# Experts with 416 places instead of 384: a fourth tile of 32 rows for each expert, and two overflow tiles instead of six

## The chip, the cores and the metric

The kernel runs on one core of one Trainium2 chip. The metric is the device time of one execution in microseconds (us), as the median of several runs. Engines are named as in the profile: PE is TensorE's matmul, PEld its weight load, DVE VectorE, ACT ScalarE, POOL GpSimd, SP SyncE.

## The reference

The first half is clustered attention over 4 batches, 8 heads, 768 positions and 64 dimensions. It gives 3072 rows of 512. The second half is a mixture of 8 experts in which each row goes to exactly one expert, and no row is dropped:

```
logits = x @ w_gate                       # x: 3072 x 512, w_gate: 512 x 8
expert_idx = np.argmax(logits, axis=1)
...
for e in range(E):                        # the rows of expert e
    h = np.maximum(x_sorted[lo:hi] @ w1[e], 0.0)   # w1[e]: 512 x 1024
    y_sorted[lo:hi] = h @ w2[e]                    # w2[e]: 1024 x 512
y = y_sorted[inv_perm]
return gate_w[:, None] * y
```

Everything is float32. How many rows an expert gets depends on the data. With the reference's inputs the eight experts get 400, 354, 531, 257, 408, 444, 274 and 404 rows.

## The kernel before

The attention stage (lines 252 to 581) works through 16 groups of a batch and two heads. Its order on each engine is written out by hand. Several of its matmuls use a part of the PE array only: `similar` (L362) puts four products of 32 output columns into four quarters of one PSUM tile, `weigh` (L463) puts two such products into two quarters and adds three rounds up, `weigh2` (L477) transposes blocks of 64 rows. The attention writes its rows, with the gate weight in a further column, to a table `x_rows` in device memory.

The routing stage (L584 to L713) counts the rows of each expert and gives each row a place. Each expert has `CAP` = 384 places, three tiles of 128. Rows beyond that go to overflow tiles of 128 rows that belong to one expert each. A product of one-hot matrices (L703) turns the places around into a table `g_idx` (for each tile a column with the numbers of the rows to be gathered) and `s_idx` (the rows of the output to be written; empty places point out of bounds and are not written). The count of overflow tiles is a value at run time; the first `XU` = 6 are written out in the program, and a loop (L797 to L807) does any further one.

The expert stage takes the groups in the order experts 0 to 7, then overflow tiles 0 to 5. For a group, `gather` fetches its rows by an indirect DMA for each tile (POOL), `turn_rows` transposes them on PE (4 transposes for a tile into `tp`, two buffers, emptied by DVE), `layer1` computes `h` for all tiles of the group at once (32 matmuls into `hp`, moving 384 columns, or 128 for an overflow tile), and `layer2` takes one tile after the other (8 matmuls of 512 columns into `zp`, two buffers, emptied by ACT with the gate weight, then an indirect DMA on POOL to the output). The order on PE is written out: layer 1 of group i, transposes of group i+1, layer 2 of group i. After them come the gather of group i+2 and the fetch of the weights of group i+3, two transfers of 2 MB on SP's queue into one of three weight buffers.

A float32 matmul stands in the trace as two records, a transpose as one.

Of the kernel before, what the change touches and what calls it, by code (L numbers as in the profile page):

```python
# [8 lines left out]
F32 = mybir.dt.float32  # L9
# [3 lines left out]
AF = mybir.ActivationFunctionType  # L13
# [6 lines left out]
BIG = float(2**60)  # L20
LAG = 2
LEAD = 14
XU = 6


def in_general(tc, ident, ident_b, first_c, first_e, wpool, q, k, v, centroids, w_gate, w1, w2, out):
# [156 lines left out]
def kernel(  # L183
# [11 lines left out]
    nc = tc.nc  # L195
    B, H, S, D = q.shape
    C = centroids.shape[1]
    P = 128
# [5 lines left out]
    N = B * S  # L204
    Dm = H * D
    E = moe_w_gate.shape[1]
    F = moe_w1.shape[2]
    DB = Dm // P
    FB = F // P
    NT = N // P  # L210
    KA = D + C
    XW = Dm + 4
    assert D == 64 and C == 16 and H * C == P and NQ % 2 == 0 and NQ * P == S and DB * P == Dm and FB * P == F

    NJ = N // E // P
    CAP = NJ * P
    NX = -(-(N - CAP) // P)
    NC = E * NJ + NX
    assert XU <= NX

    x_d = nc.dram_tensor("x_rows", (N, XW), F32, kind="Internal").ap()

    consts = ctx.enter_context(tc.tile_pool(name="consts", bufs=1))
# [3 lines left out]
    def fetch(e):  # L227
        w1 = wpool.tile([P, DB, F], F32, name="w1")
        w2 = wpool.tile([P, FB, Dm], F32, name="w2")
        nc.sync.dma_start(out=w1, in_=moe_w1[bass.ds(e, 1)].rearrange("e (a p) f -> p (e a) f", p=P))  # L230
        nc.sync.dma_start(out=w2, in_=moe_w2[bass.ds(e, 1)].rearrange("e (a p) d -> p (e a) d", p=P))
        return w1, w2
# [19 lines left out]
    with ExitStack() as actx:  # L252
# [4 lines left out]
        ap = actx.enter_context(tc.tile_pool(name="ap", bufs=4))  # L257
# [9 lines left out]
        rows = {}  # L267
# [34 lines left out]
        for i in range(2):  # L302
            t = consts.tile([P, 2 * NQ, 2, D], BF16, name=f"oh{i}")
# [289 lines left out]
    keep = consts.tile([P, E, NT], F32)  # L593
    nc.gpsimd.memset(keep, 1.0)
    nc.gpsimd.memset(keep[:, :, 0:1], 0.0)
    b1off = iota("b1off", [P, E], [[CAP, E]], -1, 0)
    b2off = iota("b2off", [P, E], [[-CAP, E]], E * CAP - CAP, 0)
    thr = iota("thr", [P, NX], [[P, NX]], CAP, 0)
    kx = iota("kx", [1, NX], [[1, NX]], 0, 0)
    iota_f = iota("iota_f", [P, P], [[1, P]], 0, 0)  # L600
    tokv = iota("tokv", [P, B, NQ], [[S, B], [1, NQ]], 1, NQ)

    g_idx = rte.tile([P, NC], I32)
    s_idx = rte.tile([P, NC], I32)
    xe = rte.tile([1, NX + 2], I32)

    with tc.tile_pool(name="sm", bufs=1) as sm, tc.tile_pool(name="rps", bufs=1, space=PSUM) as rps:
# [59 lines left out]
        gx = sm.tile([P, E, NT], F32)  # L667
        nc.vector.tensor_scalar(gx, slot, scalar1=CAP + 0.5, scalar2=None, op0=ALU.is_ge)
        nc.vector.tensor_tensor(gx, gx, b2.unsqueeze(2).to_broadcast([P, E, NT]), op=ALU.mult)
# [14 lines left out]
        oh_r = sm.tile([P, NT, P], F32)  # L684
        oh_c = sm.tile([P, NT, NC], F32)
        tok_ps = rps.tile([P, NC], F32, name="tok_ps")
        tok = tokv.rearrange("p b j -> p (b j)")
        TH = NT // 4
        for t0 in range(0, NT, TH):
            ts = slice(t0, t0 + TH)  # L690
            nc.vector.tensor_tensor(
                oh_c[:, ts, :], iota_f[:, None, :NC].to_broadcast([P, TH, NC]),
                rc[:, 1, ts].unsqueeze(2).to_broadcast([P, TH, NC]), op=ALU.is_equal,
            )
# [18 lines left out]
        nc.vector.tensor_copy(s_idx, tb)  # L713


    mctx = ExitStack()
    xg_pool = mctx.enter_context(tc.tile_pool(name="moe_x", bufs=3))
    wk = mctx.enter_context(tc.tile_pool(name="moe_wk", bufs=2))
    mps = mctx.enter_context(tc.tile_pool(name="moe_ps", bufs=3, space=PSUM))

    def gather(g):
        g["xg"] = xg_pool.tile([P, NJ, XW], F32, name="xg")
        for j in range(g["n"]):
            nc.gpsimd.indirect_dma_start(  # L724
                out=g["xg"][:, j, :], out_offset=None,
                in_=x_d[:, :], in_offset=bass.IndirectOffsetOnAxis(ap=g["gi"](j), axis=0),
            )

    def turn_rows(g):
        g["xT"] = wk.tile([P, DB, NJ * P], F32, name="xgT")  # L730
        for j in range(g["n"]):
            tp = mps.tile([P, DB, P], F32, name="tp", bufs=2)
            for c in range(DB):
                nc.tensor.transpose(tp[:, c, :], g["xg"][:, j, c * P : (c + 1) * P], ident)  # L734
            nc.vector.tensor_copy(g["xT"][:, :, j * P : (j + 1) * P], tp)  # L735

    def layer1(g):
        cols = g["n"] * P
        g["h"] = wk.tile([P, FB, NJ * P], F32, name="h_sb")
        for fb in range(FB):  # L740
            hp = mps.tile([P, NJ * P], F32, name="hp")
            for c in range(DB):
                nc.tensor.matmul(  # L743
                    hp[:, :cols], lhsT=g["w"][0][:, c, fb * P : (fb + 1) * P], rhs=g["xT"][:, c, :cols],
                    start=(c == 0), stop=(c == DB - 1),
                )
            if fb % 2 == 0:
                nc.vector.tensor_relu(g["h"][:, fb, :cols], hp[:, :cols])  # L748
            else:
                nc.scalar.activation(g["h"][:, fb, :cols], hp[:, :cols], AF.Relu)  # L750

    def layer2(g):
        for j in range(g["n"]):
            zp = mps.tile([P, Dm], F32, name="zp", bufs=2)
            for fb in range(FB):
                nc.tensor.matmul(  # L756
                    zp, lhsT=g["h"][:, fb, j * P : (j + 1) * P], rhs=g["w"][1][:, fb, :],
                    start=(fb == 0), stop=(fb == FB - 1),
                )
            zo = wk.tile([P, Dm], F32, name="zo", bufs=3)  # L760
            nc.scalar.activation(zo, zp, AF.Copy, scale=g["xg"][:, j, Dm : Dm + 1])  # L761
            ins = nc.gpsimd.indirect_dma_start(  # L762
                out=out[:, :], out_offset=bass.IndirectOffsetOnAxis(ap=g["si"](j), axis=0),
                in_=zo, in_offset=None, bounds_check=N - 1, oob_is_err=False,
            )
            if g["apart"]:
                ins = getattr(ins, "ins", ins)
                tc.declare_no_dep(ins, group="rows_out", reason="disjoint rows")
                tc.add_to_no_dep_group("rows_out", ins)

    def cols_of(t, c0):
        return lambda j: t[:, c0 + j : c0 + j + 1]

    groups = []
    for e in range(E):
        groups.append(dict(n=NJ, e=e, gi=cols_of(g_idx, e * NJ), si=cols_of(s_idx, e * NJ), apart=True))
    for x in range(XU):
        ex = nc.sync.value_load(xe[0:1, x : x + 1], min_val=0, max_val=E - 1)
        groups.append(dict(n=1, e=ex, gi=cols_of(g_idx, E * NJ + x), si=cols_of(s_idx, E * NJ + x), apart=True))
    with tc.manual_schedule():  # L780
        for i in range(2):
            gather(groups[i])
        turn_rows(groups[0])
        for i, g in enumerate(groups):
            g["w"] = weights.pop(i)
            layer1(g)
            if i + 1 < len(groups):
                turn_rows(groups[i + 1])
            layer2(g)
            if i + 2 < len(groups):  # L790
                gather(groups[i + 2])
            if i + 3 < len(groups):
                weights[i + 3] = fetch(groups[i + 3]["e"])

    nx = nc.values_load(xe[0:1, NX : NX + 1], min_val=0, max_val=NX)
    general = nc.values_load(xe[0:1, NX + 1 : NX + 2], min_val=0, max_val=1)
    with tc.If(nx > XU):  # L797
        with tc.For_i(XU, nx, 1) as i:
            ex = nc.sync.value_load(xe[0:1, bass.ds(i, 1)], min_val=0, max_val=E - 1)
            gi = wk.tile([P, 2], I32, name="gi")  # L800
            nc.vector.tensor_copy(gi[:, 0:1], g_idx[:, bass.ds(i + E * NJ, 1)])
            nc.vector.tensor_copy(gi[:, 1:2], s_idx[:, bass.ds(i + E * NJ, 1)])
            g = dict(n=1, w=fetch(ex), gi=lambda j: gi[:, 0:1], si=lambda j: gi[:, 1:2], apart=False)
            gather(g)
            turn_rows(g)
            layer1(g)
            layer2(g)  # L807
# [31 lines left out]
```

## Time and profile before

| | us |
|---|---|
| median of 3 runs (942.52 to 944.6) | 943.83 |
| the profiled execution | 942.97 |
| span of its profile, first to last instruction | 941.1 |
| PE busy | 880.3 |
| PE's weight load busy (beside PE) | 454.3 |
| DVE busy | 302.1 |
| ACT busy | 270.8 |
| POOL busy | 93.2 |

The profile describes one execution; its span is 1.9 us shorter than that execution's time, and the execution is 0.9 us shorter than the median. Busy time of an engine is the union of its instructions. The span divides by stage: attention up to about 449 us, routing and first gather up to 483 us, eight experts up to 829 us, six overflow tiles up to 931 us, and an end of 10 us in which the last rows are written and the two conditions behind the groups are read.

### The profile page before, as it was taken

The numbers are of one execution on the slowest core, as the hardware profiler recorded it, in microseconds if no ns is written. First come the engines' busy times: TensorE is split into PE (matmuls) and PEld (weight loads), VectorE is DVE, ScalarE is ACT, GpSimd is POOL, SyncE is SP. The second block draws the span as 40 slices with busy tenths as digits, with TensorE's granted clock in tenths as the row PEclk, the third lists the DMA queues.
The fourth block names the chain that finished last, engine by engine and source line by source line (L and its number), as shares of the span: only waits on it lengthen the run. The fifth ranks groups of instructions, "written<-read, shape, count | busy, mean of one in ns | idle before, by whom it ended". The sixth has DMA issues, their size and how long they took to land.

```text
span 941.1 us, 10715 instructions
## 1 busy us (share of the span) xinstructions
PE 880.3 (94%) x4367; PEld 454.3 (48%) x4367; DVE 302.1 (32%) x527; ACT 270.8 (29%) x432; POOL 93.2 (10%) x141
## 2 busy tenths in 40 slices
PE   4999999999999999999479999999999999989895
PEld 2444444444444444444445555454545455556663
DVE  2565556555554556554611010100101010001110
ACT  3645455555554555454000101001000101101110
POOL 3000000000000000000220202010120201011000
PEclk8999999999999999999669999999999999989998
DMA  7127223151235322000122424232434333256700
GB/s 159 29 52 229 51 51 119 65 174 42 51 119 207 73 51 85 2 1 1 67 68 92 155 100 144 111 135 112 154 125 180 125 126 121 100 212 217 275 18 11
DMA packets 82587, 99.00 MB, mean 105 GB/s; under 512 B 52959, under 2 KB 57055, under 8 KB 82016
## 3 DMA queue, kind: packets, MB, share of 16 engines
q1 hardware_dynamic: 76480, 77.60, 26.2%
q0 software_dynamic: 5376, 20.56, 5.7%
q8 instruction: 37, 0.61, 0.3%
q14 instruction: 22, 0.18, 0.1%
q10 hardware_dynamic: 672, 0.05, 0.0%
HBM read 85.57 MB, written 14.20 MB: 106 GB/s over the span
## 4 chain that ended last, share of the span: by engine, by line
issue 44%; PE 40%; DVE 7%; POOL 6%; ACT 1%; DMA 0%; POOLq 0%; DVEq 0%; ACTq 0%
PE sps L425 14%; PE O L445 12%; PE mps L463 4%; DVE T L437 3%; PE sps L428 3%; POOL out_dram L762 3%; POOL xg L724 3%; PE mps L342 2%; PE mps L362 1%; ACT A L430 1%; PE tok_ps L703 1%; PE mps L400 1%; DVE qk L350 1%; PE mps L373 1%; PE mps L506 1%
## 5 line engine op out<-in xcount | busy, mean ns | idle before, releaser
L743 PE MATMUL hp<-xgT,w 128*128 128x384 f32 (+1 forms) x896 | 212.2, 398 | 0.8 <-DVE xgT L735 0.8
L756 PE MATMUL zp<-w,h_sb 128*128 128x512 f32 x480 | 211.7, 600 | 0.0
L430 ACT ACTIVATE A<-sps 128x768 f32<-128x768 f32 x192 | 155.4, 811 | 80.4 <-PE sps L428 78.7
L743 PEld LDWEIGHTS hp<-xgT,w 128*128 128x128 f32 x896 | 142.1, 192 | 73.8 <-issue 7.9
L425 PE MATMUL sps<-qk 64*128 64x384 f32 x768 | 166.1, 510 | 0.0
L437 DVE TENSOR_TENSOR T<-T,A 128x768 f32<-128x768 f32 x128 | 122.5, 957 | 85.6 <-ACT A L430 78.6
L445 PE MATMUL O<-A,v_in 128*64 128x384 f32 x768 | 145.1, 499 | 0.0
L756 PEld LDWEIGHTS zp<-w,h_sb 128*128 128x128 f32 x480 | 91.7, 194 | 110.0 <-issue 110.0
L748 DVE TENSOR_SCALAR h_sb<-hp 128x384 f32<-128x384 f32 (+1 forms) x56 | 24.9, 444 | 358.9 <-PE hp L743 358.9
L425 PEld LDWEIGHTS sps<-qk 64*128 64x128 f32 x768 | 63.4, 187 | 52.2 <-issue 31.5
L445 PEld LDWEIGHTS O<-A,v_in 128*64 128x64 f32 x768 | 46.6, 136 | 79.8 <-issue 79.8
L750 ACT ACTIVATE h_sb<-hp 128x384 f32<-128x384 f32 (+1 forms) x56 | 22.3, 399 | 215.3 <-PE hp L743 215.3
L761 ACT ACTIVATE zo<-zp,xg 128x512 f32<-128x512 f32 x30 | 20.6, 687 | 221.3 <-PE zp L756 221.3
L762 POOL DMA_INDIRECT out_dram<-zo,s_idx x30 | 30.1, 1002 | 389.9 <-ACT zo L761 389.9
L428 PE MATMUL sps<-ohT 64*128 64x384 bf16 x384 | 63.2, 323 | 0.0
L433 DVE SCALAR_TENSOR_TENSOR T<-A 128x768 f32<-128x768 f32 x32 | 30.7, 959 | 93.8 <-ACT A L430 93.8
L383 POOL TENSOR_TENSOR sim<-sim,first_c 128x384 f32<-128x384 f32 x16 | 15.9, 994 | 300.6 <-DVE sim L382 300.6
L734 PE MATMUL tp<-ident,xg 128*128 128x128 f32 x120 | 19.8, 303 | 19.4 <-DMA xg<-x_rows,g_idx 17.0
L735 DVE COPY xgT<-tp 128x512 f32<-128x512 f32 x30 | 20.1, 689 | 45.5 <-PE tp L734 45.5
L428 PEld LDWEIGHTS <-ohT 64*128 64x128 bf16 x384 | 19.4, 94 | 24.9 <-issue 0.3
L724 POOL DMA_INDIRECT xg<-x_rows,g_idx x30 | 29.1, 971 | 16.3 <-issue 8.8
L734 PEld LDWEIGHTS tp<-ident,xg 128*128 128x128 f32 x120 | 14.9, 153 | 25.2 <-issue 19.3
(146 smaller groups left out, 436.6 us busy)
## 6 DMA issues: line engine op xcount, KB each, us to landing
w<-in_moe_w_dram SPq DMA_DIRECT2D x28, 2048.0 KB, 9.2
x_rows<-x POOLq DMA_DIRECT2D x4, 1548.0 KB, 5.9
q_in<-in_q_dram SPq DMA_DIRECT2D x32, 192.0 KB, 4.7
k_in<-in_k_dram SPq DMA_DIRECT2D x32, 192.0 KB, 4.7
v_in<-in_v_dram SPq DMA_DIRECT2D x16, 384.0 KB, 3.6
xg<-x_rows,g_idx POOLq DMA_INDIRECT x30, 6.8
out_dram<-zo,s_idx POOLq DMA_INDIRECT x30, 2.7
csb<-in_centroids_dram ACTq DMA_DIRECT2D x1, 32.0 KB, 1.7
```

The costliest lines, as they stand in the source:

```text
L425: nc.tensor.matmul(ps[:, a, 0:HS], lhsT=qk[g][r, 1, ks], rhs=qk[g][r, 0, qs], start=True, stop=False)
L428: nc.tensor.matmul(ps[:, a, 0:HS], lhsT=ohT[g][r, 1, ks], rhs=ohT[g][r, 0, qs], start=False, stop=True)
L430: nc.scalar.activation(A[u], ps[:, :, 0:HS], AF.Exp)
L433: nc.vector.scalar_tensor_tensor(T[g, half], in0=A[u - 1], scalar=1e-9 / P, in1=A[u], op0=ALU.add, op1=ALU.add)
L437: nc.vector.tensor_tensor(T[g, half], T[g, half], A[u], op=ALU.add)
L445: nc.tensor.matmul(O[g, half][a * D : (a + 1) * D, 0:HS], lhsT=rows[g, "v"][:, a, j, :], rhs=a_[:, a, :], start=(j == 0), stop=(j == NQ - 1),)
L463: nc.tensor.matmul(ps[half * 32 : (half + 1) * 32, 0:HS], lhsT=one_row[:, i, :] if i < 2 else wg[:, g % HP, :], rhs=t[half][:, i, :] if i ...
L724: nc.gpsimd.indirect_dma_start(out=g["xg"][:, j, :], out_offset=None, in_=x_d[:, :], in_offset=bass.IndirectOffsetOnAxis(ap=g["gi"](j), ax ...
L734: nc.tensor.transpose(tp[:, c, :], g["xg"][:, j, c * P : (c + 1) * P], ident)
L743: nc.tensor.matmul(hp[:, :cols], lhsT=g["w"][0][:, c, fb * P : (fb + 1) * P], rhs=g["xT"][:, c, :cols], start=(c == 0), stop=(c == DB - 1),)
L756: nc.tensor.matmul(zp, lhsT=g["h"][:, fb, j * P : (j + 1) * P], rhs=g["w"][1][:, fb, :], start=(fb == 0), stop=(fb == FB - 1),)
L762: ins = nc.gpsimd.indirect_dma_start(out=out[:, :], out_offset=bass.IndirectOffsetOnAxis(ap=g["si"](j), axis=0), in_=zo, in_offset=None, b ...
```

## The change

An expert has 416 places: three tiles of 128 rows and one of `RQ` = 32. Two overflow tiles are written out instead of six. In the numbering of places an expert still takes a whole number of tiles of 128 (now four, the last only used in its first 32 rows), so the index tables have 53 columns instead of 45.

The tile of 32 rows is gathered and transposed as a smaller tile. Layer 1 moves 416 columns instead of 384. In layer 2 its 8 matmuls (each 128 deep, 32 output columns, 512 moved) are dealt to four column groups of the array: group `t` adds up blocks `2t` and `2t+1` of `h` into the partitions `32t` to `32t+31` of a PSUM tile `zq`. DVE copies `zq` to `zc`, and one matmul with a constant `fold` (four 32 by 32 unit matrices on top of each other) sums the four parts. Then the 32 rows are scaled and written like those of any tile (`rows_out`).

```diff
-XU = 6
+XU = 2
+RQ = 32
...
-    CAP = NJ * P
+    CAP = NJ * P + RQ
     NX = -(-(N - CAP) // P)
-    NC = E * NJ + NX
+    NC = E * (NJ + 1) + NX
...
+    fold = consts.tile([P, RQ], F32)
+    for t in range(P // RQ):
+        nc.gpsimd.tensor_copy(fold[t * RQ : (t + 1) * RQ, :], ident[t * RQ : (t + 1) * RQ, t * RQ : (t + 1) * RQ])
...
     def gather(g):
-        for j in range(g["n"]):
+        for j, m in enumerate(g["n"]):
             nc.gpsimd.indirect_dma_start(
-                out=g["xg"][:, j, :], out_offset=None,
-                in_=x_d[:, :], in_offset=bass.IndirectOffsetOnAxis(ap=g["gi"](j), axis=0),
+                out=g["xg"][0:m, j, :], out_offset=None,
+                in_=x_d[:, :], in_offset=bass.IndirectOffsetOnAxis(ap=g["gi"](j)[0:m], axis=0),
             )
...
             for c in range(DB):
-                nc.tensor.transpose(tp[:, c, :], g["xg"][:, j, c * P : (c + 1) * P], ident)
-            nc.vector.tensor_copy(g["xT"][:, :, j * P : (j + 1) * P], tp)
+                nc.tensor.transpose(tp[:, c, 0:m], g["xg"][0:m, j, c * P : (c + 1) * P], ident[0:m, 0:m])
+            nc.vector.tensor_copy(g["xT"][:, :, j * P : j * P + m], tp[:, :, 0:m])
...
     def layer2(g):
-        for j in range(g["n"]):
+        zc = None
+        if len(g["n"]) > NJ:
+
+            zq = mps.tile([P, Dm], F32, name="zq", bufs=1)
+            n = FB * RQ // P
+            for i in range(n):
+                for t in range(P // RQ):
+                    nc.tensor.matmul(
+                        zq[t * RQ : (t + 1) * RQ, :], lhsT=g["h"][:, t * n + i, NJ * P : CAP],
+                        rhs=g["w"][1][:, t * n + i, :], start=(i == 0), stop=(i == n - 1),
+                    )
+            zc = wk.tile([P, Dm], F32, name="zc", bufs=1)
+            nc.vector.tensor_copy(zc, zq)
+        for j in range(min(len(g["n"]), NJ)):
             zp = mps.tile([P, Dm], F32, name="zp", bufs=2)
...
+            rows_out(g, j, P, zp)
+        if zc is not None:
+            zp = mps.tile([P, Dm], F32, name="zp", bufs=2)
+            nc.tensor.matmul(zp[0:RQ, :], lhsT=fold, rhs=zc, start=True, stop=True)
+            rows_out(g, NJ, RQ, zp)
```

On PE the change shows first around one expert. Before, from the first group's transposes to the second group's layer 1 (`w_750` and `w_751` are the two weight tiles of expert 0, `w_1652` the first of expert 1):

```order
L734 MATMUL tp<-ident,xg 128x128 x12
L743 MATMUL hp<-xgT,w_750 128x384 x32
L734 MATMUL tp<-ident,xg 128x128 x12
L756 MATMUL zp<-w_751,h_sb 128x512 x24
L743 MATMUL hp<-xgT,w_1652 128x384 x32
```

The same place with the change:

```order
L740 MATMUL tp<-ident,xg 128x128 x12
L740 MATMUL tp<-ident,xg 128x32 x4
L749 MATMUL hp<-xgT,w_750 128x416 x32
L740 MATMUL tp<-ident,xg 128x128 x12
L740 MATMUL tp<-ident,xg 128x32 x4
L778 MATMUL zq<-w_751,h_sb 32x512 x8
L787 MATMUL zp<-w_751,h_sb 128x512 x24
L794 MATMUL zp<-zc,fold 32x512
L749 MATMUL hp<-xgT,w_1652 128x416 x32
```

Thirteen instructions are new for each expert, and the 32 of layer 1 move 416 columns. The eight into `zq` stand ahead of the three full tiles, the one with `fold` behind them.

On PE the program's end, before, from layer 2 of expert 7 to layer 1 of the second overflow tile (`w_4719` and `w_4720` are the first overflow tile's weights; behind these rows the same three kinds of rows go on to the sixth overflow tile, the last without transposes):

```order
L756 MATMUL zp<-w_4602,h_sb 128x512 x24
L743 MATMUL hp<-xgT,w_4719 128x128 x32
L734 MATMUL tp<-ident,xg 128x128 x4
L756 MATMUL zp<-w_4720,h_sb 128x512 x8
L743 MATMUL hp<-xgT,w_4835 128x128 x32
```

With the change, from layer 2 of expert 7 on:

```order
L778 MATMUL zq<-w_4704,h_sb 32x512 x8
L787 MATMUL zp<-w_4704,h_sb 128x512 x24
L794 MATMUL zp<-zc,fold 32x512
L749 MATMUL hp<-xgT,w_4846 128x128 x32
L740 MATMUL tp<-ident,xg 128x128 x4
L787 MATMUL zp<-w_4847,h_sb 128x512 x8
L749 MATMUL hp<-xgT,w_4986 128x128 x32
L787 MATMUL zp<-w_4987,h_sb 128x512 x8
```

Four groups of 32 matmuls, 4 transposes and 8 matmuls are gone; the first and the last overflow tile stand as before.

On POOL, around the first overflow tile, before and then with the change (the rows into `out_dram` write a tile's rows, those into `xg` gather one; the gather shown here is that of the second overflow tile):

```order
L762 DMA out_dram<-zo,s_idx 3072x512 x3
L724 DMA xg<-x_rows,g_idx 128x516
L762 DMA out_dram<-zo,s_idx 3072x512
```

```order
L761 DMA out_dram<-zo,s_idx 3072x512 x4
L730 DMA xg<-x_rows,g_idx 128x516
L761 DMA out_dram<-zo,s_idx 3072x512 x2
```

The gather of the second overflow tile now stands behind four writes of expert 7 instead of three. The four copies into `fold` stand on POOL among the constants that it makes at the start of the program.

## Rows read from the trace of the kernel before

**Rows 1.** The page, busy time of PE, share of span, instructions.

```profile
PE 880.3 (94%) x4367; PEld 454.3 (48%) x4367; DVE 302.1 (32%) x527; ACT 270.8 (29%) x432; POOL 93.2 (10%) x141
```

**Rows 2.** Windows: us, busy PE, PEld, DVE, ACT, POOL (records), PEclk, DMA share, GB/s.

```profile
528.50:571.60 43.10, 42.75 (x126) 22.54 (x124) 4.21 (x7) 4.02 (x7) 5.91 (x6) 1.00 0.37 135
850.00:916.80 66.80, 59.65 (x337) 43.38 (x336) 7.44 (x20) 7.18 (x20) 7.97 (x8) 0.97 0.51 180
```

**Rows 3.** Timeline of PE for expert 1: start, us, records, idle before.

```profile
528.48 20.80 PE L743 MATMUL hp<-xgT,w 128*128 128x384 f32 x64
549.12 1.04 PE L734 MATMUL tp<-ident,xg 128*128 128x128 f32 x8
550.50 0.66 PE L734 MATMUL tp<-ident,xg 128*128 128x128 f32 x4 [0.35 <-DVE xgT L735]
551.00 20.77 PE L756 MATMUL zp<-w,h_sb 128*128 128x512 f32 x48
571.60 20.80 PE L743 MATMUL hp<-xgT,w 128*128 128x384 f32 x64
```

**Rows 4.** Timeline of PE: first, second and last overflow tile.

```profile
828.88 7.31 PE L743 MATMUL hp<-xgT,w 128*128 128x128 f32 x64
839.82 1.09 PE L734 MATMUL tp<-ident,xg 128*128 128x128 f32 x4 [3.63 <-DMA xg<-x_rows,g_idx]
840.70 9.45 PE L756 MATMUL zp<-w,h_sb 128*128 128x512 f32 x16
849.98 7.31 PE L743 MATMUL hp<-xgT,w 128*128 128x128 f32 x64
...
916.84 7.31 PE L743 MATMUL hp<-xgT,w 128*128 128x128 f32 x64
```

**Rows 5.** Timeline of PE in the attention: products of 32 columns, small transposes.

```profile
51.11 0.85 PE L362 MATMUL mps<-qk,cblk 128*32 128x384 f32 x8
51.90 0.92 PE L425 MATMUL sps<-qk 64*128 64x384 f32 x4
...
55.63 1.48 PE L463 MATMUL mps<-T,one_row 128*32 128x384 f32 x8
56.94 0.81 PE L463 MATMUL mps<-xT,wg 128*32 128x384 f32 x4
57.69 0.92 PE L425 MATMUL sps<-qk 64*128 64x384 f32 x4
...
60.95 0.40 PE L477 MATMUL mps<-ident,lsT 64*128 64x64 f32 x3
61.27 0.55 PE L506 MATMUL mps<-ident,xT 128*128 128x128 f32 x3
```

**Rows 6.** Timeline of PE's weight loads beside L463.

```profile
55.98 0.12 PEld L463 LDWEIGHTS mps<-T,one_row 128*32 128x32 f32 x2 [0.21 <-issue]
...
56.30 0.12 PEld L463 LDWEIGHTS mps<-T,one_row 128*32 128x32 f32 x2 [0.20 <-issue]
```

**Rows 7.** Timeline of POOL and PE at the first gathers.

```profile
477.73 0.95 POOL L724 DMA_INDIRECT xg<-x_rows,g_idx  x1 [0.30 <-issue]
478.98 0.95 POOL L724 DMA_INDIRECT xg<-x_rows,g_idx  x1 [0.30 <-issue]
...
481.56 1.09 PE L734 MATMUL tp<-ident,xg 128*128 128x128 f32 x4 [0.40 <-DMA xg<-x_rows,g_idx]
483.43 22.73 PE L743 MATMUL hp<-xgT,w 128*128 128x384 f32 x64 [0.78 <-DVE xgT L735]
```

**Rows 8.** Groups by line, 449 to 484 us: the one-hot product's records and loads.

```profile
L703 PE MATMUL tok_ps<-oh_c,oh_r 128*128 128x45 f32 x48 | 10.5, 423 | 6.9 <-POOL oh_c L695 6.9
...
L703 PEld LDWEIGHTS tok_ps<-oh_c,oh_r 128*128 128x128 f32 x48 | 10.3, 332 | 7.0 <-POOL oh_c L695 7.0
```

**Rows 9.** Timeline of POOL at the first overflow tile.

```profile
830.09 0.98 POOL L762 DMA_INDIRECT out_dram<-zo,s_idx  x1 [5.88 <-ACT zo L761]
831.38 0.99 POOL L724 DMA_INDIRECT xg<-x_rows,g_idx  x1 [0.30 <-issue]
```

More of the change, by code (lines that the diff above doesn't have):

```diff
@@ L595 @@
     nc.gpsimd.memset(keep[:, :, 0:1], 0.0)
-    b1off = iota("b1off", [P, E], [[CAP, E]], -1, 0)
-    b2off = iota("b2off", [P, E], [[-CAP, E]], E * CAP - CAP, 0)
+    b1off = iota("b1off", [P, E], [[(NJ + 1) * P, E]], -1, 0)
+    b2off = iota("b2off", [P, E], [[-(NJ + 1) * P, E]], E * (NJ + 1) * P - CAP, 0)
     thr = iota("thr", [P, NX], [[P, NX]], CAP, 0)
@@ L721, in gather @@
     def gather(g):
-        g["xg"] = xg_pool.tile([P, NJ, XW], F32, name="xg")
-        for j in range(g["n"]):
+        g["xg"] = xg_pool.tile([P, NJ + 1, XW], F32, name="xg")
+        for j, m in enumerate(g["n"]):
             nc.gpsimd.indirect_dma_start(
-                out=g["xg"][:, j, :], out_offset=None,
-                in_=x_d[:, :], in_offset=bass.IndirectOffsetOnAxis(ap=g["gi"](j), axis=0),
+                out=g["xg"][0:m, j, :], out_offset=None,
+                in_=x_d[:, :], in_offset=bass.IndirectOffsetOnAxis(ap=g["gi"](j)[0:m], axis=0),
             )
     def turn_rows(g):
-        g["xT"] = wk.tile([P, DB, NJ * P], F32, name="xgT")
-        for j in range(g["n"]):
+        g["xT"] = wk.tile([P, DB, CAP], F32, name="xgT")
+        for j, m in enumerate(g["n"]):
             tp = mps.tile([P, DB, P], F32, name="tp", bufs=2)
             for c in range(DB):
-                nc.tensor.transpose(tp[:, c, :], g["xg"][:, j, c * P : (c + 1) * P], ident)
-            nc.vector.tensor_copy(g["xT"][:, :, j * P : (j + 1) * P], tp)
+                nc.tensor.transpose(tp[:, c, 0:m], g["xg"][0:m, j, c * P : (c + 1) * P], ident[0:m, 0:m])
+            nc.vector.tensor_copy(g["xT"][:, :, j * P : j * P + m], tp[:, :, 0:m])
     def layer1(g):
-        cols = g["n"] * P
-        g["h"] = wk.tile([P, FB, NJ * P], F32, name="h_sb")
+        cols = sum(g["n"])
+        g["h"] = wk.tile([P, FB, CAP], F32, name="h_sb")
         for fb in range(FB):
-            hp = mps.tile([P, NJ * P], F32, name="hp")
+            hp = mps.tile([P, 512], F32, name="hp")
             for c in range(DB):
@@ L750, in layer1, with rows_out @@
                 nc.scalar.activation(g["h"][:, fb, :cols], hp[:, :cols], AF.Relu)
-    def layer2(g):
-        for j in range(g["n"]):
+    def rows_out(g, j, m, zp):
+        zo = wk.tile([P, Dm], F32, name="zo", bufs=3)
+        nc.scalar.activation(zo[0:m], zp[0:m], AF.Copy, scale=g["xg"][0:m, j, Dm : Dm + 1])
+        ins = nc.gpsimd.indirect_dma_start(
+            out=out[:, :], out_offset=bass.IndirectOffsetOnAxis(ap=g["si"](j)[0:m], axis=0),
+            in_=zo[0:m], in_offset=None, bounds_check=N - 1, oob_is_err=False,
+        )
+        if g["apart"]:
+            ins = getattr(ins, "ins", ins)
+            tc.declare_no_dep(ins, group="rows_out", reason="disjoint rows")
+            tc.add_to_no_dep_group("rows_out", ins)
+    def layer2(g):
+        zc = None
[7 more added lines that the diff above has]
+                        rhs=g["w"][1][:, t * n + i, :], start=(i == 0), stop=(i == n - 1),
+                    )
+            zc = wk.tile([P, Dm], F32, name="zc", bufs=1)
+            nc.vector.tensor_copy(zc, zq)
+        for j in range(min(len(g["n"]), NJ)):
             zp = mps.tile([P, Dm], F32, name="zp", bufs=2)
@@ L759, in layer2 @@
                 )
[L760 to L769, printed above, removed]
+            rows_out(g, j, P, zp)
[3 more added lines that the diff above has]
+            rows_out(g, NJ, RQ, zp)
     def cols_of(t, c0):
@@ L775 @@
     for e in range(E):
-        groups.append(dict(n=NJ, e=e, gi=cols_of(g_idx, e * NJ), si=cols_of(s_idx, e * NJ), apart=True))
+        groups.append(
+            dict(n=[P] * NJ + [RQ], e=e, gi=cols_of(g_idx, e * (NJ + 1)), si=cols_of(s_idx, e * (NJ + 1)), apart=True)
+        )
     for x in range(XU):
         ex = nc.sync.value_load(xe[0:1, x : x + 1], min_val=0, max_val=E - 1)
-        groups.append(dict(n=1, e=ex, gi=cols_of(g_idx, E * NJ + x), si=cols_of(s_idx, E * NJ + x), apart=True))
+        xc = E * (NJ + 1) + x
+        groups.append(dict(n=[P], e=ex, gi=cols_of(g_idx, xc), si=cols_of(s_idx, xc), apart=True))
     with tc.manual_schedule():
@@ L800 @@
             gi = wk.tile([P, 2], I32, name="gi")
-            nc.vector.tensor_copy(gi[:, 0:1], g_idx[:, bass.ds(i + E * NJ, 1)])
-            nc.vector.tensor_copy(gi[:, 1:2], s_idx[:, bass.ds(i + E * NJ, 1)])
-            g = dict(n=1, w=fetch(ex), gi=lambda j: gi[:, 0:1], si=lambda j: gi[:, 1:2], apart=False)
+            nc.vector.tensor_copy(gi[:, 0:1], g_idx[:, bass.ds(i + E * (NJ + 1), 1)])
+            nc.vector.tensor_copy(gi[:, 1:2], s_idx[:, bass.ds(i + E * (NJ + 1), 1)])
+            g = dict(n=[P], w=fetch(ex), gi=lambda j: gi[:, 0:1], si=lambda j: gi[:, 1:2], apart=False)
             gather(g)
```

## The prediction

> **What bounds the kernel now.** The page says that PE is busy for 880 of 941 us [rows 1]. That is an average, so I read the windows next. From 528.5 to 571.6 us, one expert, PE is busy 42.75 of 43.10 us with a granted clock of 1.00, the 2.4 GHz level; DVE, ACT and POOL have 4 to 6 us of work each and the DMA share is 0.37 [rows 2]. In this stage the time is PE's work, and whatever PE gets on top lengthens the kernel by as much. The timeline of PE shows how the 43.12 us of an expert are made up: layer 1 from 528.48 to 549.12, transposes to 551.00, layer 2 to 571.60 [rows 3]. Overflow tiles differ: PE is busy 59.65 of 66.80 us [rows 2], because it waits for a gather ahead of the transposes (3.63 us at the first), and at the first of them layer 2 takes 9.28 us (840.70 to 849.98) behind that wait [rows 4], where 8 of the 24 matmuls of an expert take 6.87. The change trades PE time of the second kind for PE time of the first.
>
> **Does it do what it says?** The reference's counts give 16, 147, 24, 60 and 20 rows above 384: one tile each, two for the 147, six in all. Above 416 are only 115 (of 531) and 28 (of 444): two tiles. The nearest expert, 408, is 8 rows short of a third. So the loop behind the groups stays unused.
>
> **What goes.** Of six overflow groups the first (its transposes are the next group's, its wait is for the second gather) and the last (no transposes behind it) stand as before. What goes is what lies between layer 1 of the second and layer 1 of the last: 916.84 - 849.98 = 66.9 us [rows 4]. The end of 10 us behind the last tile is the same work.
>
> **What comes, for each of eight experts, on PE.**
>
> Layer 1. 32 matmuls of 384 columns take 20.64 us, 0.645 each; 24 of 512 take 20.60, 0.858 each [rows 3]. The difference is 1.67 ns a column, so 32 columns more are 0.053 us, times 32 matmuls 1.71 us. The eight evictions into `h` grow with it, but DVE and ACT have 4 us of work in 43 [rows 2], so nothing waits.
>
> Transposes. Four of 32 rows. No row shows that shape; the nearest is the block of 64 rows of `weigh2`, three in 0.32 us with the step to the next shape (60.95 to 61.27), 0.107 each [rows 5]; four full ones take 0.50 us (550.50 to 551.00) [rows 3]. I take 0.45. The third tile already waits 0.35 us for DVE to empty the first of the two `tp` buffers [rows 3]; the fourth waits for the second, whose copy runs while the third is transposed. Bounds are 0 and 0.35; I take 0.1, since that copy follows the first directly.
>
> The change of the array's shape. A round of two 32-column products of 384 takes 0.75 us where full matmuls follow in another shape (56.94 to 57.69), 0.655 within a run of the same shape (half of 55.63 to 56.94) [rows 5]: 0.1 us for each change of shape. An expert gets five: into the small transposes, into `zq`, into the full tiles, into `fold`, into the next layer 1. Transposes are then 0.45 + 0.1 + 0.1 = 0.65.
>
> The eight matmuls into `zq`. The row that decides is `similar`: four products of 128 deep, 32 output columns and 384 moved, in four column groups, take 0.79 us to the next shape (51.11 to 51.90), where one alone would take 0.645 [rows 5]. So four run abreast, and the surcharge is 0.145. `weigh` shows that rounds that add up in the same place follow without a gap: two rounds in 1.31 us [rows 5]. Two rounds of 512 columns are 2 x 0.858 + 0.145 = 1.86 us, plus 0.1 for the change into them: 1.96. Below: 1.72. Above: the surcharge twice and every weight load in the open, 16 of at most 0.12 us [rows 6], 4.0.
>
> `zc` costs DVE one copy; it has some 20 us, the three full tiles, until `fold` wants it. Without that cover PE would wait for it, as it waits 0.78 us for a copy ahead of the first layer 1 [rows 7].
>
> The matmul with `fold`. 0.858 us and a change before and behind it, 1.06. Its `zp` buffer was emptied a tile earlier. The scaling and the write of 32 rows lie beside the next layer 1; POOL goes from 6 DMA instructions of about 1 us in an expert to 8.
>
> Together 1.71 + 0.65 + 1.96 + 1.06 = 5.4 us an expert. Eight times 1.71, 1.96 and 1.06 are 37.8; the small transposes stand seven times in this stage, 4.6.
>
> **At the seams.** The first group's fourth gather is issued at 478.98, 1.25 us behind the third, which PE met at 481.56; layer 1 began at 483.43, behind the copy of the third tile [rows 7]. The fourth should be there at about 482.8, while PE is still at the third; small transposes and copy then put layer 1 off by some 0.4 us (bounds 0.2 and 1.3). The index tables grow from 45 to 53 columns: the one-hot product's loads are busy 10.3 of its 10.5 us [rows 8], and loads don't grow; POOL's four products do, by 18%. I take 0.5 us (0.2 to 1). The gather of the second overflow tile stands behind a fourth write: before, one write and 0.3 us lay between them (830.09, 831.38) [rows 9]. As the fourth comes 1.29 us behind the third, but layer 1 also starts 1.06 later, PE's wait of 3.63 grows by 0.25. `fold`'s copies run on POOL among the constants, ahead of the first attention work that it has to wait for: nothing. Four fetches of 4 MB on SP's queue and four reads of an expert's number go; none of them was waited for.
>
> **Sum.** 37.8 + 4.6 + 0.4 + 0.5 + 0.25 = 43.5 us come, 66.9 go: 23.4 us less. The profiled execution of 942.97 us becomes 919.6; it lies 0.9 below the median, so the median goes to about **920.5 us**.
>
> **Rivals.**
>
> A, the column groups don't overlap as four and two rounds: then 8 matmuls of 0.858 are 6.86 us in place of 1.72, 5.1 an expert and 41 in all, and the kernel is slower, 961.6 us. It turns at 2.9 us more an expert, when `zq` takes 4.9 us. Against it stand the 0.79 us of `similar` [rows 5]. What it would need is a difference between that case and this: two rounds, 512 columns, weights out of `h`.
>
> B, the weight loads lie in the open. The rows speak against it: beside `weigh` two loads start every 0.32 us, at 55.98 and 56.30, while its matmuls of two groups run without a gap [rows 6]. With 16 loads of 0.12 us in a row it would be 1.9 us an expert, 15 in all, 935.9 us. The Trainium skill, "TensorE: Matmul & The Clock Gate", section "Part 3: Packing small matmuls", states that a weight load overlaps a running matmul only where the row group differs; here all products use all rows. By that rule the sum would be B's; this trace disagrees for two groups, and no run here shows four groups with a second round.
>
> C, the small tile costs more in waits than in work: the fourth tile's transposes wait a full 0.35 us more, changes of shape cost twice as much, the first gather comes late. 7 x 0.25 + 8 x 0.5 + 1 = 6.8 us: 927.
>
> D, the remaining overflow wait falls away or the clock holds over it: of the 21.1 us between the first two overflow groups' layer 1, up to 6.6 are the wait and the slower layer 2 behind it. 914 us. But its gather stands later, not earlier, so this is unlikely.
>
> E, a third overflow tile after all, by the loop: an overflow tile takes 66.9 / 4 = 16.7 us with its weights fetched ahead; in the loop the 4.2 MB come with nothing beside them, at the 180 GB/s of the overflow stage [rows 2] another 23. That is 960. The counts exclude it but for an error in them.
>
> **How the numbers follow.** The forecast has 0.72, its own range 916 to 925. C has 0.11, B 0.07, A 0.05, D 0.04, E 0.01. About 0.2% (1.9 us) is what can be told from no change here. A and E are slower, 0.06; all others are faster, 0.93; 0.01 is left for a case between B and A. With all lower bounds the added work is 38 us (no change of shape, no wait, 0.65 at the seams; 915), with all upper ones 64 (4.0 for `zq`, twice the price of a change and a full wait at the transposes, 2.8 at the seams; 941). The range from 913 to 934 takes in C and D and leaves out A, B and E.
>
> **What would show it.** In the profile after: an expert's period of 48.5 us instead of 43.12; layer 1 at 22.35; the records into `zq` within about 1.9 us; `fold` under 1.1; two overflow tiles from the first layer 1 to the end in about 45.6 us (21.4 + 24.3); PE's wait for the second overflow gather still there. Records into `zq` one after another over 6.9 us would be A; gaps of load time between them, B; a DVE wait at the fourth tile near 0.4, C.

## The result and the profile after

| | median, us | ratio to the kernel before, 95% interval |
|---|---|---|
| before | 943.17 (939.35 to 944.6, 4 runs) | |
| changed | 912.70 (912.07 to 913.29, 4 runs) | 0.9683 [0.9653, 0.9713] |

The change gains 30.5 us, 3.2%. The forecast was 920.5, so the direction is right and the time is 7.8 us shorter than forecast, 0.3 us under the low end of the range; as a ratio to the kernel before, which the forecast had at 943.83 us, it is 913.9 us and just inside. It lies below the forecast's own range (916 to 925) and beside rival D's 914, which had a chance of 0.04. The page of the changed kernel, part 1 (compare [rows 1]):

```profile
PE 859.7 (94%) x4207; PEld 415.5 (46%) x4207; DVE 303.9 (33%) x523; ACT 269.9 (30%) x420; POOL 100.6 (11%) x153
```

PE is still what bounds it, with 20.6 us less work; the span went from 941.1 to 910.7 us, 30.4 less. So some 10 us of the gain are time in which PE stood still before.

The timeline of PE in the changed kernel for expert 1, which answers to [rows 3] (start, length, line, records, idle before):

```profile
533.83 22.61 PE L749 MATMUL hp<-xgT,w 128*128 128x416 f32 x64
556.28 1.04 PE L740 MATMUL tp<-ident,xg 128*128 128x128 f32 x8
557.67 1.03 PE L740 MATMUL tp<-ident,xg 128*128 128x128 f32 x8 [0.35 <-DVE xgT L741]
558.63 1.92 PE L778 MATMUL zq<-w,h_sb 128*32 128x512 f32 x16
560.48 20.87 PE L787 MATMUL zp<-w,h_sb 128*128 128x512 f32 x48
581.28 1.04 PE L794 MATMUL zp<-zc,fold 128*32 128x512 f32 x2
582.26 22.61 PE L749 MATMUL hp<-xgT,w 128*128 128x416 f32 x64
```

From one layer 1 to the next it is 48.43 us, where 48.5 were forecast. Layer 1 takes 22.45 (1.81 more than before), the transposes 2.35 (0.47 more), the eight products into `zq` 1.85, the three full tiles of layer 2 20.80 (0.20 more), `fold` 0.98. The third and fourth tile's transposes stand in one row without a gap between them: the fourth does not wait for its buffer. The same stretch with all engines shows the weight loads; the first line is that of the small transposes, the others are those of the column groups:

```profile
558.27 0.32 PEld L740 LDWEIGHTS tp<-ident,xg 32*128 32x128 f32 x4 [0.18 <-DVE xgT L741]
...
558.63 0.16 PEld L778 LDWEIGHTS zq<-w,h_sb 128*32 128x32 f32 x8
...
559.08 0.13 PEld L778 LDWEIGHTS zq<-w,h_sb 128*32 128x32 f32 x4 [0.30 <-issue]
559.51 0.13 PEld L778 LDWEIGHTS zq<-w,h_sb 128*32 128x32 f32 x4 [0.30 <-issue]
```

Eight loads are busy for 0.16 us together, then four at a time in 0.13, 0.43 apart, while the products run: four groups load side by side and the second round's loads are hidden. The Trainium skill, "TensorE: Matmul & The Clock Gate", section "Part 3: Packing small matmuls", states that loads overlap running matmuls only where the row group differs; all sixteen records here use all rows, and the trace disagrees. The same section of the Trainium skill also lets a load into the background weight buffer go ahead of running matmuls; whether that is what happens here no run shows.

The overflow stage, timeline of PE, which answers to [rows 4]:

```profile
870.97 7.41 PE L749 MATMUL hp<-xgT,w 128*128 128x128 f32 x64
878.22 0.60 PE L740 MATMUL tp<-ident,xg 128*128 128x128 f32 x4
878.66 7.03 PE L787 MATMUL zp<-w,h_sb 128*128 128x512 f32 x16
885.53 7.31 PE L749 MATMUL hp<-xgT,w 128*128 128x128 f32 x64
```

Here is the difference to the forecast. The transposes follow layer 1 without a wait, layer 2 runs at full clock, and the group takes 14.56 us where 21.10 stood before and 21.35 were forecast. The gather that PE used to wait for now lands early. The windows show what lay beside it; first those of the kernel before, around its first overflow tile and around its fifth, at whose transposes PE did not wait (columns as in [rows 2]: us, busy PE, PEld, DVE, ACT, POOL, PEclk, DMA share, GB/s):

```profile
829.00:840.00 11.00, 7.37 (x66) 7.21 (x65) 1.17 (x4) 1.79 (x5) 1.97 (x2) 0.94 0.86 293
...
902.40:909.60 7.20, 7.20 (x66) 7.20 (x65) 1.17 (x4) 1.52 (x4) 2.00 (x2) 1.00 0.16 44
```

and of the changed kernel, around its first overflow tile:

```profile
871.00:878.30 7.30, 7.30 (x66) 7.30 (x66) 1.17 (x4) 1.51 (x4) 2.85 (x3) 1.00 0.24 78
```

Before, the DMA engines were 86% busy while the gather was under way, because 2 MB of weights of the third overflow tile came in beside it (issued at 829.07) and, from 836.22 on, a first part of the fourth's. In the changed kernel no group follows whose weights would have to come, and the share is 0.24. The gather's time from issue to landing, for the tile `xg` in these stretches, is 8.3 us before around the first overflow tile:

```profile
DMA to landing us min/median/max: 8.3/8.3/8.3
```

and 3.6 in the changed kernel:

```profile
DMA to landing us min/median/max: 3.6/3.6/3.6
```

The start, timeline of PE in the changed kernel, which answers to [rows 7]:

```profile
481.77 1.65 PE L740 MATMUL tp<-ident,xg 128*128 128x128 f32 x8 [0.45 <-DMA xg<-x_rows,g_idx]
483.89 24.13 PE L749 MATMUL hp<-xgT,w 128*128 128x416 f32 x64 [0.47 <-issue]
```

The fourth tile is there when the third is transposed, and layer 1 starts 0.46 us later than before.

### The profile page after: what moved, and what is told of

The parts are those of the page before. It is cut to its first block, busy times and chain, and to the rows that moved or that the text cites. A ratio compares the mean times of both kernels' runs of the same rounds, so it can differ in the third digit from the quotient of the medians.

```text
span 910.7 us, 10362 instructions
## 1 busy us (share of the span) xinstructions
PE 859.7 (94%) x4207; PEld 415.5 (46%) x4207; DVE 303.9 (33%) x523; ACT 269.9 (30%) x420; POOL 100.6 (11%) x153
## 4 chain that ended last, share of the span: by engine, by line
PE 41%; issue 41%; DVE 7%; POOL 7%; ACT 2%; DMA 1%; POOLq 0%; DVEq 0%; ACTq 0%
PE sps L426 14%; PE O L446 12%; PE mps L464 4%; DVE T L438 3%; POOL out_dram L761 3%; PE sps L429 3%; POOL xg L730 3%; PE mps L343 3%; PE mps L363 2%; ACT A L431 1%; PE tok_ps L704 1%; PE mps L401 1%; DVE qk L351 1%; PE mps L374 1%; PE mps L507 1%
## 5 line engine op out<-in xcount | busy, mean ns | idle before, releaser
L749 PE MATMUL hp<-xgT,w 128*128 128x416 f32 (+1 forms) x640 | 197.1, 469 | 0.5 <-issue 0.5
L787 PE MATMUL zp<-w,h_sb 128*128 128x512 f32 x416 | 181.0, 594 | 0.0
L749 PEld LDWEIGHTS hp<-xgT,w 128*128 128x128 f32 x640 | 111.9, 192 | 87.5 <-issue 87.5
L754 DVE TENSOR_SCALAR h_sb<-hp 128x416 f32<-128x416 f32 (+1 forms) x40 | 21.3, 532 | 330.7 <-PE hp L749 330.7
L787 PEld LDWEIGHTS zp<-w,h_sb 128*128 128x128 f32 x416 | 78.2, 190 | 101.4 <-issue 101.2
L760 ACT ACTIVATE zo<-zp,xg 128x512 f32<-128x512 f32 (+1 forms) x34 | 23.3, 685 | 198.2 <-PE zp L787 196.2
L756 ACT ACTIVATE h_sb<-hp 128x416 f32<-128x416 f32 (+1 forms) x40 | 18.8, 469 | 208.1 <-PE hp L749 208.1
L741 DVE COPY xgT<-tp 128x512 f32<-128x512 f32 (+1 forms) x34 | 18.9, 593 | 30.5 <-PE tp L740 30.5
L740 PE MATMUL tp<-ident,xg 128*128 128x128 f32 (+1 forms) x136 | 19.5, 281 | 8.8 <-DMA xg<-x_rows,g_idx 6.4
L343 PE MATMUL mps<-ident,q_in 128*128 128x128 f32 x96 | 18.2, 307 | 6.5 <-DVE qk L351 6.3
```

Source lines behind the costliest of these rows:

```text
L343: nc.tensor.transpose(ps[:, i * P : (i + 1) * P], rows[g, "qk"[w]][:, j].rearrange("p a d -> p (a d)"), ident)
L749: nc.tensor.matmul(hp[:, :cols], lhsT=g["w"][0][:, c, fb * P : (fb + 1) * P], rhs=g["xT"][:, c, :cols], start=(c == 0), stop=(c == DB - 1),)
L787: nc.tensor.matmul(zp, lhsT=g["h"][:, fb, j * P : (j + 1) * P], rhs=g["w"][1][:, fb, :], start=(fb == 0), stop=(fb == FB - 1),)
```

## The experiments

All ratios are to the kernel before, run on the same chip. The theory after the result: in the kernel before, the gather of the next overflow tile came late because a fetch of weights was under way beside it, and with the fetches the waits went. The rival: the gather reads 28 different rows now (the others are empty places that all read row 0) and read 128 before, and is quicker for that.

**One fetch put back (e1_fetch_back).**

```diff
             if i + 3 < len(groups):
                 weights[i + 3] = fetch(groups[i + 3]["e"])
+            elif i == E - 1:
+                fetch(E - 1)
```

> The changed kernel with one more fetch of 4.2 MB of weights behind expert 7, which nothing reads. Theory (the overflow tile's gather was late before because a weight fetch went through the DMA engines beside it): the gather beside the first overflow tile lands about 8 us after its issue instead of 3.6, PE waits some 3.9 us at its transposes, the granted clock falls behind the wait, and the time is 6 to 8 us longer, about 920 us, which is what was predicted for the change. Rival (the gather is faster because it reads 28 different rows instead of 128): no wait, 912.7 us.

Measured: 915.39 us (915.33 to 917.12), ratio 0.9710 [0.9675, 0.9744]. Timeline of PE:

```profile
871.71 7.41 PE L749 MATMUL hp<-xgT,w 128*128 128x128 f32 x64
881.12 0.75 PE L740 MATMUL tp<-ident,xg 128*128 128x128 f32 x4 [2.00 <-DMA xg<-x_rows,g_idx]
881.66 8.68 PE L787 MATMUL zp<-w,h_sb 128*128 128x512 f32 x16
890.18 7.31 PE L749 MATMUL hp<-xgT,w 128*128 128x128 f32 x64
```

The wait is back by a fetch alone, with the slower layer 2 behind it, but it is 2.00 us and not 3.9; the gather takes 6.8 us to land and not 8.3. The medians differ by 2.7 us, less than half of the 6 to 8 that the theory had put on it. The run shown took 917.12 us and the other three 915.33 to 915.45: the difference is about what this layer 2 lost (8.68 us for 7.03), so the others need not have had it.

**The overflow tiles in the other order (e2_overflow_order).**

```diff
-    for x in range(XU):
+    for x in reversed(range(XU)):
```

> The changed kernel with its two overflow tiles in the other order, so that the gather beside the first one reads 115 different rows and not 28. Theory (weight fetch beside the gather): nothing changes, 912.7 us, no wait of PE ahead of the last transposes. Rival (the number of different rows): the gather takes 4 us longer, PE waits about 3.5 us and the time is 4 to 7 us longer.

Measured: 912.75 us (911.99 to 913.37), ratio 0.9680 [0.9645, 0.9715]. Timeline of PE behind layer 1 of the first overflow tile, at 871.77:

```profile
879.02 0.60 PE L740 MATMUL tp<-ident,xg 128*128 128x128 f32 x4
```

No wait, with 115 different rows; the gather lands in 3.3 us. The rival falls for a gather by itself.

**Both together (e8_fetch_and_order).** The two edits above in one kernel.

> The changed kernel with one unread fetch behind expert 7 and the two overflow tiles in the other order: the gather beside the fetch now reads 115 different rows, where the same fetch with 28 rows left a wait of 2.00 us. Theory (the gather lands when the fetch beside it has landed, some 10.2 us after that fetch was issued, whatever it reads): again a wait near 2.0 us, 915 to 917 us. Rival (under contention the number of different rows counts, and makes the 1.6 us by which the wait before was longer): a wait near 3.6 us, 917 to 919 us.

Measured: 915.03 us (913.88 to 917.53), ratio 0.9711 [0.9678, 0.9743]. Timeline of PE:

```profile
870.10 7.41 PE L749 MATMUL hp<-xgT,w 128*128 128x128 f32 x64
879.55 0.65 PE L740 MATMUL tp<-ident,xg 128*128 128x128 f32 x4 [2.04 <-DMA xg<-x_rows,g_idx]
880.04 7.03 PE L787 MATMUL zp<-w,h_sb 128*128 128x512 f32 x16
```

The wait is 2.04 us with 115 different rows as it was 2.00 with 28: their number does not count beside a fetch either. What counts is the fetch. SP issued it at 869.22, and PE's transposes start 10.33 us later; in e1 it was 870.84 and 10.28 later. Timeline of SP in e8:

```profile
869.22 0.38 SPq L232 DMA_DIRECT2D w<-in_moe_w_dram  x1
```

Before the change the fetch was issued at 829.07 and the transposes came 10.75 us later. The fetch is released by the last full tile of layer 2. Before, layer 1 followed at once (828.88, 0.19 ahead of the fetch's record); with the change `fold` stands between, and layer 1 starts 0.88 after it. So 1.07 of the 1.6 us by which the wait is shorter than before is a head start that the fetch now has on PE, and 0.10 is the longer record of layer 1 (7.41 for 7.31). The other 0.4, by which the gather lands sooner after the fetch's issue, stay open.

**Two fetches put back (e1b_two_fetches).** `elif i <= E:` in place of `elif i == E - 1:`.

> The changed kernel with two more fetches of weights that nothing reads, behind expert 7 and behind the first overflow tile, so that the same transfers stand beside the gather as before the change (one fetch alone brought back a wait of 2.00 us and a landing of 6.8 us, before it was 3.63 and 8.3). Theory: the first half of the second fetch starts while the gather is under way and delays it further, the wait is 3 to 4 us, the time about 919 us. Rival (the rest of the delay comes from the number of different rows, 28 now and 128 before): the wait stays at 2 us, 915.5 us.

Measured: 917.11 us (915.61 to 917.6), ratio 0.9718 [0.9693, 0.9744]. The wait is 2.03 us:

```profile
882.04 0.66 PE L740 MATMUL tp<-ident,xg 128*128 128x128 f32 x4 [2.03 <-DMA xg<-x_rows,g_idx]
882.53 7.03 PE L787 MATMUL zp<-w,h_sb 128*128 128x512 f32 x16
```

The expected 3 to 4 us did not come. When the gather landed, some 0.4 MB of the second fetch had moved beside it (2.52 MB on the queue of the fetches from 871.7 to 882.0, where e1 moved the 2.10 MB of one transfer alone), nearly as much as in the kernel before (2.56 MB from 829.0 to 839.7), and the wait is that of e1. So the second fetch does not make the part of the wait that e1 lacks; that the rival named the same 2 us is no support for its reason, the number of rows, which e8 rules out. The time is 4.4 us above the changed kernel's, but in the profile 1.2 of that is there before the first layer 1 (485.11 against 483.89). Layer 2 behind the wait ran at full clock here and in e8, and slower in e1, after the same 2 us.

**The kernel before without the fetches (e3_before_no_fetch).**

```diff
-            if i + 3 < len(groups):
+            if i + 3 <= E:
                 weights[i + 3] = fetch(groups[i + 3]["e"])
+            elif i + 3 < len(groups):
+                weights[i + 3] = g["w"]
```

> The kernel before, in which overflow tiles two to six take the weights that lie in the buffers instead of fetching their own, so their rows are computed with the wrong expert's weights; all matmuls, gathers and writes stay. Theory: all four waits of PE in the overflow stage (3.63, 2.10, 2.92 and 2.13 us) go, and with them the slow layer 2 behind the first; each overflow tile takes 14.5 us, and the time is about 15 us shorter, 928 us. Rival (number of rows): the first wait stays, 10 us or less are gained.

Measured: 927.99 us (926.73 to 928.21), ratio 0.9839 [0.9803, 0.9875]. All waits are gone, with 128 different rows in the first of the gathers and 19 to 60 in the others. Windows of its first and second overflow tile:

```profile
829.70:844.20 14.50, 14.50 (x85) 10.62 (x84) 1.86 (x5) 1.80 (x5) 1.97 (x2) 1.00 0.12 37
844.20:858.60 14.40, 14.40 (x85) 10.62 (x84) 1.86 (x5) 1.80 (x5) 2.00 (x2) 1.00 0.08 22
```

PE is busy throughout and its clock stays at the 2.4 GHz level. From the first overflow tile's layer 1 to the last's it is 72.25 us (829.75 to 902.00), before 87.96. This settles that the fetches made the waits: taking them away is worth 15.2 us to the kernel before.

**The kernel before with earlier gathers (e4_before_early_gather).** Four buffers for `xg`, three gathers ahead of the loop, and:

```diff
-            if i + 2 < len(groups):
-                gather(groups[i + 2])
+            if i + 3 < len(groups):
+                gather(groups[i + 3])
```

> The kernel before with each group's gather issued one group earlier (a fourth gather buffer), weights fetched as before. Theory: the gathers still collide with the fetches but have 14 us more, so no wait is left: about 928 us as without the fetches. Rival (PE waits for the weights themselves, or the gathers slow the fetches down): the waits move to layer 1 and little is gained. If the theory holds, 15 of the change's 30 us could be had without it.

Measured: 927.46 us (927.27 to 927.97), ratio 0.9840 [0.9805, 0.9875]. As fast as without the fetches, with all of them in place; the overflow tiles follow each other in 14.45 us. Timeline of PE:

```profile
828.90 7.31 PE L743 MATMUL hp<-xgT,w 128*128 128x128 f32 x64
836.04 0.60 PE L734 MATMUL tp<-ident,xg 128*128 128x128 f32 x4
836.48 7.03 PE L756 MATMUL zp<-w,h_sb 128*128 128x512 f32 x16
843.35 7.31 PE L743 MATMUL hp<-xgT,w 128*128 128x128 f32 x64
```

So the weights themselves do not keep PE waiting in these stages, and half of the change's gain could be had by issuing the gathers earlier. Against a kernel before that has this, the change is worth 14.8 us, 927.46 - 912.70.

**What the change adds by itself (e5_six_tiles).** `XU = 6` in the changed kernel.

> The changed kernel with six overflow tiles written out, four of them empty. It has all that the change adds and nothing of what it removes. By the sum of the prediction 66.9 us come back, and by the collision of gathers and fetches the first wait with its slow layer 2 as well, some 7: about 986 us, 43 slower than before. Rival (the added work is cheaper than the seven-fold period shows, and the gain comes from elsewhere): clearly under 980.

Measured: 982.57 us (980.7 to 986.63), ratio 1.0428 [1.0397, 1.0460], 39.4 us slower than before. The first wait came back with 1.81 us and the next three with 2.53, 2.04 and 1.35, 7.7 us in all where the kernel before has 10.8, and no layer 2 ran slow:

```profile
881.35 0.66 PE L740 MATMUL tp<-ident,xg 128*128 128x128 f32 x4 [1.81 <-DMA xg<-x_rows,g_idx]
...
898.55 0.63 PE L740 MATMUL tp<-ident,xg 128*128 128x128 f32 x4 [2.53 <-DMA xg<-x_rows,g_idx]
```

From the first overflow tile's layer 1 to the last's it is 80.87 us (872.13 to 953.00), before 87.96. Those 7.1 us less hide a part of what the change adds: the experts' stage is 41.8 us longer (484.92 to 872.13), 41.6 in the changed kernel. The time lies between the 986 us that was expected and the 980 below which the rival put it.

The second to fourth of these waits say more of the gather. The tiles that are gathered there are empty, all 128 places read row 0, and PE waits all the same. The transposes come 9.65, 9.15 and 8.46 us after the fetch's issue (888.90, 906.08 and 922.76), while the write that stands ahead of the gather carries 115, 28 and no rows. In the kernel before it is 10.75, 9.21, 10.04 and 9.24 us with 128, 16, 128 and 19 rows written (the last of each series has no further fetch behind it). So what else moves beside the gather seems to count as well as the fetch; no run varied the write by itself.

**One column group in place of four (e6_one_group).**

```diff
-            n = FB * RQ // P
-            for i in range(n):
-                for t in range(P // RQ):
...
+            for fb in range(FB):
+                nc.tensor.matmul(
+                    zq[0:RQ, :], lhsT=g["h"][:, fb, NJ * P : CAP], rhs=g["w"][1][:, fb, :],
+                    start=(fb == 0), stop=(fb == FB - 1),
+                )
+            rows_out(g, NJ, RQ, zq)
```

> The changed kernel with the small tile's layer 2 in a single column group: eight matmuls of 32 columns one after another into the first 32 partitions, and no matmul with fold. By the prices of the prediction 8 x 0.858 = 6.86 us stand in place of 1.85 + 0.97, so 4.0 us an expert and 32 in all come on top: about 945 us, no gain at all over the kernel before. Rival (products of 32 columns are quicker than full ones, or the four groups don't matter): under 930.

Measured: 944.80 us (943.9 to 945.84), ratio 1.0018 [1.0002, 1.0035]. Timeline of PE, the small tile's layer 2 of the first expert and what follows it:

```profile
511.63 7.05 PE L776 MATMUL zq<-w,h_sb 128*32 128x512 f32 x16
518.61 20.87 PE L784 MATMUL zp<-w,h_sb 128*128 128x512 f32 x48
```

One after another the products take 6.98 us, against 1.85 for the four groups. The overlap is worth 32.1 us with `fold` paid for; without it the whole change would be no gain.

**The small tiles of four experts as one (e7_shared_small).** The 32 places of four experts share a tile of 128 rows and one column of the index tables: one gather, four full transposes, copies of 32 columns to each expert's `xT`, and after the fourth expert

```diff
-            nc.tensor.matmul(zp[0:RQ, :], lhsT=fold, rhs=zc, start=True, stop=True)
-            rows_out(g, NJ, RQ, zp)
+            for t, zc in enumerate(smalls[q]["zc"]):
+                nc.tensor.matmul(zp[t * RQ : (t + 1) * RQ, :], lhsT=fold, rhs=zc, start=True, stop=True)
+            rows_out(smalls[q], 0, zp)
```

> A version meant to beat both: the 32-row tiles of four experts are one tile of 128 rows. One gather, four full transposes, one scaling and one write serve four experts; each expert keeps its own products into its quarter sums, and the four matmuls with fold run side by side in four column groups after the fourth expert. Per expert 0.46 us of small transposes and 0.97 of fold go (11 us), twice 0.5 and twice 1.1 come, the start changes by half a microsecond: some 7 us shorter than the changed kernel, 905.5 us. Rival (the waits of the shared gather and of the added copies eat it): 910 to 914.

Measured: 903.70 us (903.17 to 906.12), ratio 0.9579 [0.9558, 0.9601]: 9.0 us shorter than the changed kernel. Timeline of PE, an expert within a group of four and the end of its fourth expert:

```profile
583.18 22.51 PE L782 MATMUL hp<-xgT,w 128*128 128x416 f32 x64
...
630.05 22.51 PE L782 MATMUL hp<-xgT,w 128*128 128x416 f32 x64
...
654.38 0.66 PE L759 MATMUL tp<-ident,xs 128*128 128x128 f32 x4
...
677.62 1.06 PE L829 MATMUL zp<-zc,fold 128*32 128x512 f32 x8
678.62 22.61 PE L782 MATMUL hp<-xgT,w 128*128 128x416 f32 x64
```

A plain expert takes 46.87 us, the fourth 48.57, and four folds side by side 1.00. The experts' stage, first layer 1 to the first overflow tile's, is 378.8 us where the changed kernel has 387.1. At the start something is lost again: the shared tile's gather, issued at 480.25, lands late, PE waits 1.59 us for it, and layer 1 begins at 487.06. Why its transposes start only 5.3 us after its issue was not tried.

## Why the prediction was right, and where it was off

- **PE bounds the experts and all that is added counts in full.** Right: 48.43 us for 48.5. The terms below miss by up to 0.2 us each, and the misses cancel: 5.31 us more an expert for 5.38. The sum of the experts' stage was 42.4 us; measured are 41.6 (387.08 from the first layer 1 to the first overflow tile's, before 345.45).
- **Layer 1** was put at 1.71 us more and takes 1.81: the step between layer 1's matmuls is 0.70 us, as extrapolated, and a change of shape ahead of it is in the 22.45 (in e6, where layer 1 follows full tiles, it is 22.34).
- **The small transposes** were put at 0.65 and cost 0.47. The wait of 0.1 at the second `tp` buffer is not there.
- **The change into the full tiles** is one of the five changes of shape that the prediction lists, but has no term of its own in its sum. The three full tiles take 20.80 us for 20.60 (560.48 to 581.28), and 20.71 in e6, where no change follows them: about 0.1 us at each end.
- **The eight matmuls into `zq`** were put at 1.96 with the change into them and take 1.85. The row of four products in the attention was the right one to read. Rivals A and B are out: e6 shows what A would have been.
- **`fold`** was put at 1.06 and takes 0.98; its cover for the copy to `zc` holds.
- **What goes**, 66.9 us between two rows of PE, was right as a difference of starts. It contains 7.2 us of waits (2.10 + 2.92 + 2.13) and nearly a microsecond of a slower layer 2, which the prediction took as the overflow tiles' own price; that made no difference to the sum. Timeline of PE in the kernel before:

```profile
859.38 0.63 PE L734 MATMUL tp<-ident,xg 128*128 128x128 f32 x4 [2.10 <-DMA xg<-x_rows,g_idx]
...
876.95 1.09 PE L734 MATMUL tp<-ident,xg 128*128 128x128 f32 x4 [2.92 <-DMA xg<-x_rows,g_idx]
877.83 7.95 PE L756 MATMUL zp<-w,h_sb 128*128 128x512 f32 x16
...
895.06 0.63 PE L734 MATMUL tp<-ident,xg 128*128 128x128 f32 x4 [2.13 <-DMA xg<-x_rows,g_idx]
```

- **The seams, the step that failed.** "Before, one write and 0.3 us lay between them ... PE's wait of 3.63 grows by 0.25." The wait was taken as the gather's own time, to be moved with its issue. It belonged to the fetch beside the gather (e3: no fetch, no wait). "Four fetches of 4 MB on SP's queue ... go; none of them was waited for" was true of the fetches and overlooked that the gather waited behind them. The term is -6.5 us (14.56 against 21.10) in place of +0.25, and with it nearly all of the gap: the span is 7.0 us shorter than forecast, of which this is 6.8, the experts' stage 0.8, the start 0.4, while the end, from the last write's issue, is 0.9 longer (10.0 us for 9.1), which stays unexplained. Of the prediction's signs, "PE's wait for the second overflow gather still there" is the one that did not come.
- **Rival D** was this case, at 914 us. It was held unlikely because the gather stands later on POOL, which is so and did not matter. That the range held is due to its having been drawn down to 913 to take D in; the reckoning behind the 920.5 kept the wait. The trace before had the evidence: four of five gathers in the overflow stage were waited for, at a DMA share of 0.78 to 0.90, and the one without a fetch beside it, in the window of share 0.16 above, was not.

The e1 family shows a limit of the theory too: by the medians a fetch put back costs 2.7 us (e1) and 2.3 us (e8) of the 6.5. The remainder is the head start (1.07 us of wait), 0.10 us of layer 1, 0.4 us that stay open, and slower matmuls behind the wait (layer 2 lost 2.4 us before, 1.65 in the profile of e1, nothing in e1b and e8; the transposes 0.4 before).

## What to carry to other kernels

A wait has to be priced by what lands last, not by the instruction that it stands at: when a change removes transfers, look which other transfers ran beside them, and compare one that had no company. A DMA that nobody waits for can still be what everybody waits for, by way of a small one beside it; here, issuing the small one a group earlier cost one buffer and gave as much as removing the fetches.

A narrow product can be made to pay by dealing its depth to the column groups and adding the parts up with a small matmul: here that was the whole gain (e6). The next thing to share was the fixed work around it, over several narrow products (e7).

## What the runs showed of the hardware

- In the overflow stage a gather of 128 rows of 2 KB landed 3.3 to 3.9 us after its issue by itself (e2, the changed kernel, the kernel before, e3), and 6.8 to 8.3 us where PE waited for it, beside a fetch of 2 MB that was issued 2.3 to 3.5 us earlier. A gather just ahead of that stage, also beside a fetch, took 6.5 us before (issued at 789.70) and 5.5 in the changed kernel (826.99); nobody waited for it. At the waits before the change and in e1 and e8 the fetches took 9.3 to 11.5 us to land, and the gather landed with them, at most 0.9 us sooner, with 28 different rows as with 115. The fetch of e8, issued at 869.22, where PE's transposes start at 879.55:

```profile
DMA to landing us min/median/max: 10.4/10.4/10.4
```

The Trainium skill, "DMA: Bandwidth & Descriptors", section "Queues, rings and completion order", states that each DMA engine takes turns between its queues a packet at a time. That fits a gather that gets only a share, and gives no time for it.

- Four column groups, two rounds and sixteen records took 1.85 us where the same products in one group took 6.98: 3.8 times.
- The granted clock after a wait of some 2 us is not settled by the length of the wait: layer 2 took 8.68 us in e1 (granted clock 0.80 on average) and 7.03 in e1b and e8 (1.00), after waits of 2.00, 2.03 and 2.04. In the kernel before it took 9.45 (0.74) after 3.63, 7.95 (0.88) after 2.92 and 7.03 after 2.10 and 2.13; in e5 7.03 after 2.53.
